# A second level of Strassen's algorithm in one GEMM of a retention + feed-forward kernel, with its weights streamed in 256 KB pieces

## The chip, the cores and the metric

The kernel runs on one core of one Trainium2 chip, in fp32. The metric is the device time of one execution in microseconds (us). "Span" is the time between the first and the last record of a profiled execution; it is 2 to 3 us shorter than the time of the same run.

TensorE does the matrix products; the trace lists each of its matmuls with a load of one operand, the weight, as an instruction of its own. In this kernel VectorE and ScalarE do the elementwise work, GpSimd a little of it, and SyncE issues the DMA transfers. The products are added up in buffers named banks (of the memory PSUM), and the program lets a bank be written again only when whoever reads it is done.

## The reference, cut to what matters

```python
def _attn_ref(q, k, v):                      # B, H, S, D = 4, 8, 768, 64
    for t in range(S):
        state = gamma * state + np.einsum('bhd,bhe->bhde', k[:, :, t], v[:, :, t])
        y[:, :, t] = scale * np.einsum('bhd,bhde->bhe', q[:, :, t], state)
    return y
def _moe_ref(x, w_in, w_out):                # x: 3072 x 512
    h = x @ w_in                             # 512 x 2048: the first GEMM
    g = np.where(h > 0.0, h, np.exp(np.minimum(h, 0.0)) - 1.0)      # ELU
    return g @ w_out                         # 2048 x 512: the second GEMM
```

The retention's output y, with its heads side by side, is x.

## The kernel before

The 3072 tokens go through in six blocks of 512. Block 1 (`tb = 0`) does its two GEMMs plainly. Blocks 2 to 6 do both with one level of Strassen's algorithm (in Winograd's form): a product of 2 x 2 quarters takes 7 multiplications of quarters for 8, and pays with additions. Sums of weights are formed once, sums of tokens for every block.

One generator serves both GEMMs. It interleaves the 7 products with their additions. `kept` is a ScalarE copy out of PSUM, `plus` a VectorE addition of PSUM and a kept copy:

```python
def strassen(product, use, between):
    yield
    pa = bank("a")                  # two banks "a", one "b", one "d"
    product(1, pa, True)
    m1 = kept(pa)
    yield
    pb = bank("b")
    product(2, pb, True)
    use("C11", plus(pb, m1))
    yield
    product(6, pa, False)           # accumulates on product 1
    u2 = kept(pa)
    yield
    pd = bank("d")
    product(7, pd, True)
    yield
    product(5, pa, False)
    u4 = kept(pa)
    use("C22", plus(pd, u4))
    yield "gap"
    product(3, pa, False)
    use("C12", pa)
    yield
    product(4, pd, False)           # on the same bank d
    use("C21", plus(pd, u2))
```

In the second GEMM a product is 16 matmuls of 128 x 128 weights and 256 columns. Its weights, already combined, come from a scratch in DRAM, 1 MB at a time, through three buffers. In the first GEMM, `use` is the ELU: two ScalarE activations and one VectorE operation.

```python
def second(tb, gqs):
    def product(j, ps, begin):
        name = {1: "C11", 2: "C21", 3: "C22", 4: "C11", 5: "T1", 6: "C11", 7: "T3"}[j]
        ws = fetched.pop((tb, j))
        for f in range(NF):                                        # 8
            for d in range(2):
                nc.tensor.matmul(
                    ps[:, d, :], lhsT=ws[:, f, d * P : (d + 1) * P], rhs=gqs[f // 2][name][:, f % 2, :],
                    ...
                )
        ...   # fetch the weights three products ahead; update C11 after products 2 and 6
```

The next block's retention runs in the gaps between these products: five bursts of small TensorE work (64 x 64 matmuls), namely scores, states and three steps of outputs. The scores are 128 such passes, which run four abreast. The first product is emitted before the last two products of the first GEMM (`tail`), so that TensorE does not wait for the last ELU.

## Time and profile before

The time before is 676.14 us, the median of three runs (674.76 to 676.36).

| before | value |
|---|---|
| span of the profiled run | 672.2 us |
| TensorE busy, and share of the chain that ended last | 97%, 97% |
| VectorE busy | 47% |
| mean DMA rate | 140 GB/s |
| one product of the second GEMM | 6.91 us, 7 in a block |
| TensorE's wait for another engine in blocks 3 to 6 | one, at the very end |

The prediction shows the lines. The end of a matmul in the profile is modelled, so busy time and the bracket "[idle before]" understate a stop by the modelled tail. Where a stop's length matters, I take the start of one matmul to the start of the next and subtract the usual pace; this I call start to start.

### The profile page before, as it was taken

The page shows a single profiled execution, that of the slowest core. Times are in us where ns is not written, and L with a number is a line of the kernel's source. Part 1 is how long each engine was busy: PE and PEld are TensorE (multiplying, and loading weights), DVE is VectorE, ACT ScalarE, POOL GpSimd, SP SyncE. Part 2 cuts the span into 40 slices and gives each one's busy share as a digit, 9 for nine tenths or more (in the row PEclk, how much of TensorE's full clock was granted, in tenths as well). Part 3 has the DMA queues.
Part 4 walks back from the last instruction along what each step waited for, and adds up shares of the span by engine and source line. Part 5 has one row for each costly group of instructions (what it writes and reads, how often), then busy time and mean ns, then how long its engine had stood idle before and what let it go on. Part 6 is the DMA issues. An engine that isn't in the chain of part 4 may idle for free.

```text
span 672.2 us, 12402 instructions
## 1 busy us (share of the span) xinstructions
PE 654.7 (97%) x5472; PEld 530.3 (79%) x5472; DVE 319.0 (47%) x529; ACT 209.1 (31%) x336; POOL 25.2 (4%) x28
## 2 busy tenths in 40 slices
PE   4899999999999999999999999999999999999997
PEld 4664445458888888888888888888888888888886
DVE  5698688566736224445313554503443612444400
ACT  7477642015540004441002542001453100444100
POOL 1001100001100001100000200000200000000000
PEclk9899999999999999999999999999999999999999
DMA  8547967249003458003347301445601335200441
GB/s 342 224 157 288 345 212 262 116 149 385 29 25 118 128 157 326 4 0 108 119 128 281 119 0 63 142 141 162 247 0 59 91 121 157 79 1 0 140 127 47
DMA packets 51941, 94.12 MB, mean 140 GB/s; under 512 B 2224, under 2 KB 39088, under 8 KB 49840
## 3 DMA queue, kind: packets, MB, share of 16 engines
q1 hardware_dynamic: 51888, 93.33, 40.5%
q8 instruction: 43, 0.70, 0.4%
q14 instruction: 10, 0.08, 0.0%
HBM read 78.64 MB, written 14.68 MB: 139 GB/s over the span
## 4 chain that ended last, share of the span: by engine, by line
PE 97%; DMA 1%; DVE 0%; issue 0%; SPq 0%; ACT 0%
PE pa L516 21%; PE pa L480 21%; PE pd L516 11%; PE pd L480 10%; PE hp L379 6%; PE pb L516 5%; PE pb L480 5%; PE pa L395 4%; PE kv L268 2%; PE pb L395 2%; PE pd L395 2%; PE y L316 2%; PE y L292 2%; PE sc L246 2%; PE pa L366 1%; DMA qk<-in_qkv_dram 1%
## 5 line engine op out<-in xcount | busy, mean ns | idle before, releaser
L516 PE MATMUL pa<-g,ws 128*128 128x256 f32 x640 | 142.8, 381 | 0.7 <-ACT m L432 0.7
L437 DVE TENSOR_TENSOR h<-pd,m 128x512 f32<-128x512 f32 x50 | 34.6, 692 | 215.8 <-ACT m L432 137.6
L516 PEld LDWEIGHTS pa<-g,ws 128*128 128x128 f32 x640 | 120.5, 190 | 17.8 <-ACT m L432 1.1
L432 ACT COPY m<-pa 128x512 f32<-128x512 f32 x75 | 43.3, 578 | 263.2 <-PE pa L516 170.4
L516 PE MATMUL pd<-g,ws 128*128 128x256 f32 x320 | 71.5, 382 | 0.0
L516 PEld LDWEIGHTS pd<-g,ws 128*128 128x128 f32 x320 | 60.1, 190 | 8.4
L355 ACT ACTIVATE r<-r 128x512 f32<-128x512 f32 x96 | 60.7, 632 | 3.1
L354 ACT ACTIVATE r<-h 128x512 f32<-128x512 f32 x60 | 37.9, 632 | 61.8 <-DVE h L437 61.8
L357 DVE SCALAR_TENSOR_TENSOR g<-r,h 128x512 f32<-128x512 f32 x60 | 42.7, 712 | 14.5 <-ACT r L355 14.5
L220 POOL TENSOR_TENSOR kvn<-kvn,vf 128x512 f32<-128x512 f32 x20 | 23.2, 1161 | 458.1 <-DMA kvn<-in_qkv_dram 314.1
L480 PE MATMUL pa<-xb,w_a 128*128 128x256 f32 x160 | 37.8, 379 | 0.0
L480 PE MATMUL pd<-xt,w_s 128*128 128x256 f32 x160 | 37.8, 379 | 0.0
L480 PE MATMUL pa<-xb,w_s 128*128 128x256 f32 x160 | 37.8, 379 | 0.0
L480 PE MATMUL pb<-xb,w_a 128*128 128x256 f32 x160 | 37.8, 379 | 0.0
L480 PE MATMUL pa<-xt,w_s 128*128 128x256 f32 x160 | 37.8, 379 | 0.0
L480 PE MATMUL pa<-xt,w_b 128*128 128x256 f32 x160 | 37.8, 379 | 0.0
L480 PE MATMUL pd<-xt,w_b 128*128 128x256 f32 x160 | 37.8, 379 | 0.0
L516 PE MATMUL pb<-g,ws 128*128 128x256 f32 x160 | 35.3, 379 | 0.0
L480 PEld LDWEIGHTS pa<-xb,w_a 128*128 128x128 f32 x160 | 30.4, 190 | 4.6 <-issue 0.5
L480 PEld LDWEIGHTS pb<-xb,w_a 128*128 128x128 f32 x160 | 30.4, 190 | 4.1
L480 PEld LDWEIGHTS pa<-xt,w_b 128*128 128x128 f32 x160 | 30.4, 190 | 4.1
L480 PEld LDWEIGHTS pd<-xt,w_b 128*128 128x128 f32 x160 | 30.4, 190 | 4.1
(93 smaller groups left out, 744.0 us busy)
## 6 DMA issues: line engine op xcount, KB each, us to landing
ws<-scratch_dram SPq DMA_DIRECT2D x35, 1024.0 KB, 5.8
wraw<-in_w_dram SPq DMA_DIRECT2D x16, 1024.0 KB, 5.7
qk<-in_qkv_dram SPq DMA_DIRECT2D x24, 512.0 KB, 9.2
kvn<-in_qkv_dram SPq DMA_DIRECT2D x24, 512.0 KB, 9.2
out_dram<-h SPq DMA_DIRECT2D x20, 256.0 KB, 5.8
scratch_dram<-w_s SPq DMA_DIRECT2D x8, 512.0 KB, 7.1
scratch_dram<-so SPq DMA_DIRECT2D x8, 512.0 KB, 3.6
out_dram<-ot SPq DMA_DIRECT2D x4, 256.0 KB, 2.2
```

The costliest lines, as they stand in the source:

```text
L220: eng.tensor_tensor(out=kv[:, 1], in0=kv[:, 1], in1=vf[:, i].unsqueeze(2).to_broadcast([C, H, D]), op=ALU.mult)
L246: nc.tensor.matmul(sc[a][rows(sub), x, p, :], lhsT=qk[rows(a), 1, p, rows(sub)], rhs=qk[rows(a), 0, p, rows(sub)], start=True, stop=True, ...
L268: nc.tensor.matmul(kvs[sub][rows(a), x, p, :], lhsT=kv[rows(sub), 0, 2 * p + a, :], rhs=kv[rows(sub), 1, 2 * p + a, :], start=True, stop=T ...
L354: nc.scalar.activation(r, h, AF.Relu, scale=-1.0)
L355: nc.scalar.activation(r, r, AF.Exp, scale=-1.0)
L357: later.append(lambda: nc.vector.scalar_tensor_tensor(g, r, -1.0, h, ALU.add, ALU.max))
L379: nc.tensor.matmul(hp, lhsT=w[n][:, fi, j // 2, j % 2, :], rhs=xb[:, j, :], start=(j == 0), stop=(j == 3))
L395: nc.tensor.matmul(ops[d], lhsT=wo[:, row, d * P : (d + 1) * P], rhs=gs[row * NF + f], start=(f == 0 and row == 0), stop=(f == NF - 1 and ...
L432: nc.scalar.copy(m, ps)
L437: nc.vector.tensor_tensor(out=h, in0=ps, in1=m, op=ALU.add)
L480: nc.tensor.matmul(ps[:, fi, :], lhsT=w[:, fi, j2, :], rhs=x[:, j2, :], start=(begin and fi == 0 and j2 == 0), stop=(j2 == 1), skip_group_ ...
L516: nc.tensor.matmul(ps[:, d, :], lhsT=ws[:, f, d * P : (d + 1) * P], rhs=gqs[f // 2][name][:, f % 2, :], start=(begin and f == 0 and d == 0 ...
```

## The change

The intent is to apply Strassen's idea once more, inside each of the 7 products of the second GEMM, from the third block on: 49 small products of 4 matmuls with 128 columns. That is 392 passes of TensorE in place of 224 passes of twice the width. VectorE and ScalarE pay for it with sums of operands and of results. In block 2 the kernel forms the sums of weights once and stores them to a second scratch. Then the 49 weight pieces of every block are streamed, 256 KB each, through eleven buffers.

```diff
+    def combine_w_out(j, ws):                       # in block 2 only, once for each product
+        a11, a21, a12, a22 = (ws[:, 4 * k : 4 * k + 4, P * d : P * d + P] for k in range(2) for d in range(2))
+        s12, s34 = (t4.tile([P, 2, 4, P], FP32, name="so", tag="t4") for _ in range(2))
+        tt(s12[:, 0], a21, a22, ALU.add)
...
+            nc.sync.dma_start(
+                scratch2[j - 1, :, 1024 * k : 1024 * k + 1024], x.rearrange("p k f d -> p (k f d)")
+            )
+    RING = 11
+    def fetch_small():
+        tb, j, k = to_fetch.pop(0)
+        t = ring.tile([P, 4, P], FP32, name="wq", tag="wq")
+        if k in (1, 2, 4):                          # pieces that are plain weights
...
+            nc.sync.dma_start(t, scratch[f : f + 4, :, col : col + P].rearrange("f p d -> p f d"))
+        else:
+            nc.sync.dma_start(t.rearrange("p f d -> p (f d)"), scratch2[j - 1, :, 512 * n : 512 * n + 512])
+    def second_twice(tb, behind_last):
+        def inputs(j):                              # VectorE: sums of operands of product j
+            sub(t[:, 0], b12, b11)
+            sub(t[:, 1], b22, t[:, 0])
+            sub(t[:, 2], b22, b12)
+            sub(t[:, 3], b21, t[:, 1])
...
+        def inner(j):                               # the seven small products of product j
+            product(j, 1, pa, True)
+            m1 = copy(pa)                           # ScalarE
+            product(j, 2, pb, True)
+            add(res[:, 0, 0], pb, m1)               # VectorE
+            yield
+            product(j, 6, pa, False)
+            u2 = copy(pa)
+            product(j, 7, pd, True)
+            product(j, 5, pa, False)
+            add(res[:, 1, 1], pd, copy(pa))
+            yield
+            product(j, 3, pa, False)
+            nc.scalar.copy(res[:, 0, 1], pa)
+            product(j, 4, pd, False)
+            add(res[:, 1, 0], pd, u2)
+            sum_up(j, ...)                          # VectorE: the outer sums
...
+        for at, j in enumerate(ORDER2):
+            cur = inner(j)
+            next(cur)                               # (j, 1), (j, 2)
+            if j == 1:
+                yield "tail"                        # the first GEMM's last two products
+            for _ in before:                        # (j-1, 3), (j-1, 4)
+                pass
+            if j == 2:
+                next_input(2)                       # the update of C11
+            if j == 5:
+                next_input(6)
+            if at + 1 < 7:
+                inputs(ORDER2[at + 1])
+            else:
+                behind_last()
+            next(cur)                               # (j, 6), (j, 7), (j, 5)
+            before = cur
+            yield j                                 # a burst of the next block's retention
```

Below, (j, k) is the small product k of the product j; j-1 is the product before j in the order 1, 2, 6, 7, 5, 3, 4. The pool of 20 buffers for ELU results also became fixed tiles.

## The prediction

> **What bounds the kernel now.** I read the engine shares and the chain first, to learn which engine sets the end; then the groups by form, for durations; then the timeline and the windows, for the pace. The page of the kernel before, engine shares and chain:
>
> ```profile
> PE 654.7 (97%) x5472; PEld 530.3 (79%) x5472; DVE 319.0 (47%) x529; ACT 209.1 (31%) x336; POOL 25.2 (4%) x28
> ...
> PE 97%; DMA 1%; DVE 0%; issue 0%; SPq 0%; ACT 0%
> ```
>
> TensorE carries 97% of the span and 97% of the chain, so only less PE time, or a new PE wait, moves the end. Groups by form (busy us, mean ns, then idle before them):
>
> ```profile
> L516 PE MATMUL pa<-g,ws 128*128 128x256 f32 x640 | 142.8, 381 | 0.7 <-ACT m L432 0.7
> L516 PEld LDWEIGHTS pa<-g,ws 128*128 128x128 f32 x640 | 120.5, 190 | 17.8 <-ACT m L432 1.1
> ...
> L437 DVE TENSOR_TENSOR h<-pd,m 128x512 f32<-128x512 f32 x50 | 34.6, 692 | 215.8 <-ACT m L432 137.6 <-PE pd L480 44.6 <-PE pd L516 33.6
> ...
> L279 DVE TENSOR_TENSOR xt<-kv,xt 128x256 f32<-128x256 f32 x32 | 13.6, 424 | 2.2 <-ACT xt L277 0.8
> ```
>
> L516 is the second GEMM. Its pa, pb and pd rows hold 640+160+320 = 1120 matmuls; the code issues 5 blocks x 7 products x 16 = 560. So one fp32 matmul is two passes, each with its own weight load. The mean of 381 ns is not the pace, since passes overlap. That is read off the timeline, here the first with PE alone, the second with weight loads alone:
>
> ```profile
> 315.01 2.10 PE L246 MATMUL sc<-qk 64*64 64x64 f32 x128
> 317.04 7.17 PE L516 MATMUL pa<-g,ws 128*128 128x256 f32 x32
> ```
>
> ```profile
> 335.31 0.30 PEld L516 LDWEIGHTS pa<-g,ws 128*128 128x128 f32 x2
> ```
>
> A product of 32 passes that follows another takes 6.91 us in the chain in order of time, so **216 ns per pass**; block by block the second GEMM costs 7 x 6.91 = 48.4 us. The windows of one block's second part (retention of the next block woven in) and of a first part:
>
> ```profile
> 208.90:252.80 43.90, 43.90 (x659) 38.14 (x658) 12.51 (x25) 1.76 (x3) 0.00 (x0) 1.00 0.46 139
> 252.80:304.60 51.80, 51.80 (x242) 45.60 (x241) 23.93 (x36) 23.50 (x40) 4.36 (x4) 1.00 0.29 107
> ```
>
> The columns are window, length, then busy us of PE, PEld, DVE, ACT, POOL. In the second part VectorE works 12.5 of 43.9 us. It has plenty of room today, and PE has no gap at all.
>
> **What the Trainium skill says.** "TensorE: Matmul & The Clock Gate", Back-to-back issue gap, says that in a stream of weight load and matmul pairs the spacing is set by both, and that narrow matmuls feel it: 81 ns at 128 columns where an isolated one needs 56. The trace cannot test 128 columns; at 256 the loads (190 ns each) hide inside the 216 ns pace, as PE shows no gap. "Perfetto Trace Analysis", Optimizing Tensor Performance, Matmuls: larger matmuls are more efficient than smaller ones. The change goes the other way. "DMA: Bandwidth & Descriptors", Bandwidth, gives 0.95 us for 64 KB and 6.15 us for 1 MB. The trace has 5.8 us for 1 MB of ws and 2.2 us for 256 KB of out<-ot, which agrees.
>
> **Part 1, matmuls: the gain.** In blocks 3 to 6 of six (tb = 2..5) each of the 7 products becomes 7 smaller ones of 4 matmuls with 128 columns: 49 x 4 x 2 = 392 passes for 7 x 16 x 2 = 224. Break-even is 48.4 us / 392 = 123 ns per pass. What is the pace at 128 columns? Matmul: 216 = 256 columns at 0.833 ns (213.3) + 2.5, so 128 columns need 109. Weight load: in the last fence two loads of 128 columns span 0.30 us, 190 of which is the second, so the second began about 0.11 us after the first; the loads overlap one another. The 64-column matmuls tell whether load and matmul of equal width really run side by side: 128 passes in four quadrants follow the product at 315.01 and give way at 317.04, 2.03 us for 32 waves, 63 ns with the changeover; the individual starts in the steady part are 58 ns apart, which is 53.3 + 5. I therefore take 106.7 + 5 = **112 ns** (estimate), and 392 x 0.1117 = 43.8 us. Gain 4.6 us per block, **18.2 us for four blocks**. A one-to-one split would give 7/8; 12.5% of 48.4 is 6.0, and the narrower pass eats 1.5 of it.
>
> **Part 2, VectorE: what it costs.** Per block the second part now holds: 7 x 4 operand subtractions of 128x512 at 0.69 = 19.3; three PSUM adds of 128x128 per product, 21 x 0.29 (from 424 at 256 and 692 at 512: 156 + 1.05 ns per element) = 6.1; outer sums 7 x 0.69 = 4.8; the update of C11, 8 x 0.69 = 5.5 (as before); the next block's retention and combine_x, some 12. That is 48 us beside about 52 us of PE (43.8 + 8.2 of retention matmuls). VectorE goes from 28% of the window to over 90%. It does not become the bound in sum, but it works in order, and the PSUM bank d is released by adds queued behind long work. I laid the queue out by hand, taking 0.89 us per small product, 0.2 us until its result can be read, 0.27 us for the ScalarE copy.
> - Normal step: after product (j-1,4), 0.2 + 0.29 + 0.69 + 2.75 (inputs of the next product) + 0.33 = 4.3 us until bank d may be accumulated on again; PE has 6 products = 5.35 us of other work. No stall.
> - Start of the part: the copy of u2 sits behind two ELU activations of the first GEMM's last tile (stall 0.75), and inputs(2) waits for that tile, so (1,4) waits 0.7. **1.4 us**.
> - Second product, with the C11 update (2.75 more) and then four score masks (2.7): (6,7) waits 0.5. Before (4,7) the xb multiplies (2.7) hold the queue: 0.75. **1.3 us**.
> - The last block has no retention to hide behind: the C11 update leaves 6.3 against 5.35 twice, plus 0.25 from three sums: 2.2 + 1.4 = **3.6 us**.
> Sum: 3 x 2.7 + 3.6 = 11.7 us. The end of the program gains two more waits on one bank and one more add, 0.8 us.
>
> **Part 3, weights.** 49 pieces of 256 KB per block are 12.8 MB for 7.3 MB before, fetched as a buffer falls free, eleven deep. In a stretch without retention PE eats one per 0.89 us, 294 GB/s. In the timeline's busiest stretches the ws loads (1 KB packets) ran at 383 GB/s by the windows view. Pieces that come from the first scratch have 512-byte packets, three in seven, so I put the mix near 330 (estimate from the per-packet times of 84 ns for 2 KB and 46 ns for 1 KB). Ten pieces of lead are 8.9 us against 2.2 us of landing plus at most 3 us in which the queue stands behind an output store. **Hidden.**
>
> **Part 4, the one-time cost.** Block 2 adds 28 combining subtractions (19.4 us of VectorE in a window where it is mostly idle) and 7 MB of stores; the ring is filled during the following first GEMM, 48 us. Nothing on the path. Fixed tiles in place of the 20-buffer pool: the built order shows waits by region (the middle of a product waits for the last tile's ELU), so no stall in the first GEMM.
>
> **Sum.** 676.1 - 18.2 + 11.7 + 0.8 = **670.4 us**, ratio 0.991.
>
> **Rivals.**
> 1. VectorE's queue stalls less than I laid out, because the pieces shift and slack grows: only the fixed start of 1.4 us per block stays. Then 676.1 - 18.2 + 6.4 = 664. For it: small products give six products of slack. Against: 48 of 52 us busy leaves no room for the retention's bursts.
> 2. Weight loads do not hide at 128 columns. At 123 ns per pass nothing is gained in the matmuls, giving 689 with the stalls; at the load's full 190 ns it would be 74.5 us per block, +104 us, 790. Against the extreme: the two loads within 0.30 us and the 64-column waves.
> 3. The weight stream falls behind (small packets, one in-order queue that also waits for output stores). If PE ran at 250 GB/s in the second part, a piece takes 1.05 us, 51.4 us per block: +3 us instead of -4.6, some 690. Against: eleven buffers, and retention work that gives 8 us per block to catch up.
>
> **Range and chances.** The pace (109 to 114 ns) moves the time by -4 to +4 us; the stalls by -6 to +7. I predict 670 us, range 661 to 681. Faster by over 2% needs 662.6, so stalls under 5 us: chance 0.14. Slower by over 2% needs rival 2 or 3: 0.07. Within 2%: 0.79.
>
> **What would show it.** In the profile after: eight passes per small product starting 0.89 us apart (right) or 1.0 and more (rival 2); PE idle before the new matmuls of 10 to 14 us, released by VectorE adds and ScalarE copies (right) or by DMA into wq (rival 3); VectorE near 90% busy in the second part. I am wrong if the PE gaps are under 5 us, or if the small products run at another pace while nothing waits.

## The result, and the profile after

The changed kernel takes 666.62 us, the median of four runs (665.87 to 668.91), beside 675.45 us for the kernel before. The ratio is **0.9875** (95% interval 0.9846 to 0.9904): within 2%, and 3.4 us under the predicted 670. All ratios here divide the mean time of one kernel's runs by that of the other's runs of the same rounds, so they are not quite the ratios of the quoted medians.

Lines of the page of the changed kernel, in the order of the page: engine shares, the chain, the new matmuls with idle time, the weight stream.

```profile
PE 640.9 (96%) x6144; PEld 538.9 (81%) x6144; DVE 434.7 (65%) x769; ACT 228.3 (34%) x432; POOL 23.7 (4%) x28
...
PE 87%; DVE 8%; issue 2%; DMA 1%; ACT 0%; SPq 0%; DVEq 0%
...
L611 PE MATMUL pd<-ts,wq 128*128 128x128 f32 x448 | 60.3, 278 | 0.6 <-DVE res L623 0.3
L611 PE MATMUL pa<-ts,wq 128*128 128x128 f32 x448 | 59.6, 276 | 1.3 <-ACT ms L619 1.3
...
wq<-scratch_dram SPq DMA_DIRECT2D x196, 256.0 KB, 4.2
```

VectorE has gained 115.7 us of work and TensorE has lost 13.8. The chain now runs 8% of its way through VectorE, and 2% through "issue": time in which TensorE waited for nothing that the profile knows. Before, that share was 0%.

The timeline of TensorE in block 3 shows what happened. The first columns are start and length; the bracket is the idle time before, and what ended it.

```profile
303.21 1.05 PE L611 MATMUL pa<-ts,wq 128*128 128x128 f32 x8
304.16 1.16 PE L611 MATMUL pd<-ts,wq 128*128 128x128 f32 x8
305.64 1.16 PE L611 MATMUL pa<-ts,wq 128*128 128x128 f32 x8 [0.32 <-ACT ms L619]
306.63 1.06 PE L611 MATMUL pa<-gC,wq 128*128 128x128 f32 x8
307.53 1.06 PE L611 MATMUL pb<-gC,wq 128*128 128x128 f32 x8
308.42 1.06 PE L611 MATMUL pa<-gC,wq 128*128 128x128 f32 x8
309.54 1.16 PE L611 MATMUL pd<-ts,wq 128*128 128x128 f32 x8
...
313.31 1.73 PE L261 MATMUL sc<-qk 64*64 64x64 f32 x101
315.65 0.68 PE L261 MATMUL sc<-qk 64*64 64x64 f32 x27 [0.61 <-issue]
```

Three things are to be seen.
1. **The pace.** From 306.63 to 307.53 to 308.42 the small products start 0.893 us apart: 8 passes of 111.6 ns.
2. **The start of the part.** (1,5) starts at 305.64, which is 1.48 us after (1,7) at 304.16: 0.48 us late beyond the 1.0 us of a product whose first weight load does not hide (some 0.10 us). It awaited the copy of u2. Then (1,4) starts at 309.54, 1.12 us after its predecessor: 0.23 us late, waiting for the addition that frees bank d. Three of the products there have such an unhidden first load (0.10 us each), and (1,7) itself starts 0.06 us late, 0.36 us together.
3. **A stop that nothing explains.** The 128 scores passes of the burst, which before took 2.10 us in one piece, break off after 101 and go on 0.61 us later ("issue"; 0.77 us start to start). There are five such stops in the profile, all in retention bursts or just after one: 0.77, 0.96, 0.87, 1.19 and 0.76 us, **4.5 us** in all. The profile before has none.

Where the copy of u2 stood is seen in ScalarE's timeline of the same kernel, and the pace of VectorE in its own:

```profile
304.14 0.63 ACT L369 ACTIVATE r<-h 128x512 f32<-128x512 f32 x1 [1.19 <-DVE h L448]
304.80 0.63 ACT L370 ACTIVATE r<-r 128x512 f32<-128x512 f32 x1
305.34 0.25 ACT L619 COPY ms<-pa 128x128 f32<-128x128 f32 x1
...
310.95 2.49 DVE L526 TENSOR_TENSOR gC<-gT,gC 128x512 f32<-128x512 f32 x4
```

The copy (L619) runs behind two ELU activations of the first GEMM's last tile, and these waited 1.19 us for a VectorE sum. In the last line four VectorE operations of 128 x 512 take 2.49 us together, 0.62 us each with the end of the last one counted in. From start to start such operations of the changed kernel, one behind the other, are **0.60 to 0.61 us** apart, although the listing gives one of them 0.69.

### The profile page after: what moved, and what is told of

The parts are those of the page before. It is cut to its first block, busy times and chain, and to the rows that moved or that the text cites. A ratio compares the mean times of both kernels' runs of the same rounds, so it can differ in the third digit from the quotient of the medians.

```text
span 664.6 us, 14658 instructions
## 1 busy us (share of the span) xinstructions
PE 640.9 (96%) x6144; PEld 538.9 (81%) x6144; DVE 434.7 (65%) x769; ACT 228.3 (34%) x432; POOL 23.7 (4%) x28
## 4 chain that ended last, share of the span: by engine, by line
PE 87%; DVE 8%; issue 2%; DMA 1%; ACT 0%; SPq 0%; DVEq 0%
PE pa L491 20%; PE pa L611 12%; PE pd L491 9%; PE pd L611 7%; PE hp L392 6%; PE pb L491 5%; PE pa L406 4%; PE pa L547 4%; DVE ts L600 3%; PE pb L611 2%; PE pd L547 2%; PE pb L406 2%; PE pd L406 2%; PE y L331 2%; PE sc L261 2%
## 5 line engine op out<-in xcount | busy, mean ns | idle before, releaser
L619 ACT COPY ms<-pa 128x128 f32<-128x128 f32 x84 | 22.2, 264 | 123.7 <-PE pa L611 119.1
L611 PE MATMUL pd<-ts,wq 128*128 128x128 f32 x448 | 60.3, 278 | 0.6 <-DVE res L623 0.3
L611 PE MATMUL pa<-ts,wq 128*128 128x128 f32 x448 | 59.6, 276 | 1.3 <-ACT ms L619 1.3
L611 PEld LDWEIGHTS pa<-ts,wq 128*128 128x128 f32 x448 | 54.8, 192 | 2.2 <-ACT ms L619 2.0
L611 PEld LDWEIGHTS pd<-ts,wq 128*128 128x128 f32 x448 | 54.5, 192 | 2.3 <-DVE res L623 1.9
L611 PE MATMUL pa<-gC,wq 128*128 128x128 f32 x384 | 52.0, 278 | 0.4 <-ACT ms L619 0.4
L372 DVE SCALAR_TENSOR_TENSOR gC<-r,h 128x512 f32<-128x512 f32 x60 | 42.7, 712 | 10.3 <-ACT r L370 10.3
L611 PEld LDWEIGHTS pa<-gC,wq 128*128 128x128 f32 x384 | 47.2, 192 | 1.7 <-ACT ms L619 0.5
L623 DVE TENSOR_TENSOR res<-pd,ms 128x128 f32<-128x128 f32 x56 | 16.1, 287 | 33.7 <-PE pd L611 31.9
L491 PEld LDWEIGHTS pd<-xt,w_s 128*128 128x128 f32 x160 | 30.4, 190 | 4.1
```

The source lines that it names most:

```text
L372: later.append(lambda: nc.vector.scalar_tensor_tensor(g, r, -1.0, h, ALU.add, ALU.max))
L491: nc.tensor.matmul(ps[:, fi, :], lhsT=w[:, fi, j2, :], rhs=x[:, j2, :], start=(begin and fi == 0 and j2 == 0), stop=(j2 == 1), skip_group_ ...
L611: nc.tensor.matmul(ps, lhsT=w[:, f, :], rhs=ts[j][k][:, f, :], start=(begin and f == 0), stop=(f == 3), skip_group_check=True,)
L619: nc.scalar.copy(m, ps)
```

## The experiments

All of them edit the changed kernel, except before_traffic, which edits the kernel before. Two questions stood at the outset. What are the unexplained stops? The theory: TensorE consumes instructions at twice the rate (a small product of 8 matmuls with their 8 loads takes 0.893 us, so 256 instructions last 14.3 us; before, a product of 64 instructions took 6.91 us, so 256 lasted 27.6 us), and its fetch of instructions, a DMA transfer too, is held up by the weight stream. The DMA view of the kernel before and that of the changed kernel list an instruction queue q8 (packets, MB, share):

```profile
q8 instruction: 43, 0.70, 0.4%
```

```profile
q8 instruction: 49, 0.80, 0.5%
```

The packets are of 16 KB. TensorE has 11,036 records before and 12,499 after (matmuls, loads and its few control instructions), which is 257 and 255 to a packet. So I took q8 for TensorE's instruction fetch, some 256 instructions to a packet. At the outset this was an inference; the section on why the prediction was right, part 3, has what bears it out. A burst of 128 scores with their loads uses up 256 instructions in 2 us. The rivals: the stream alone, or the denser use of instructions alone. The second question was what the waits on ScalarE and VectorE are worth.

The results at a glance. "Stops" are stops over 0.3 us with no releaser, in the profiled run, start to start:

| run | ratio to before (95%) | stops | median us |
|---|---|---|---|
| the change | 0.9875 (0.9846, 0.9904) | 5, 4.5 us | 666.62 |
| no_stream (wrong result) | 0.9802 (0.9785, 0.9819) | 0 | 661.44 |
| before_traffic | 1.0029 (1.0012, 1.0046) | 0 | 676.38 |
| split_retention | 0.9883 (0.9867, 0.9900) | 0 | 666.61 |
| both_orders | 0.9944 (0.9919, 0.9969) | 4, 5.0 us | 670.99 |
| early_copy | 0.9881 (0.9864, 0.9898) | 3, 3.4 us | 666.43 |
| late_inputs | 0.9892 (0.9871, 0.9912) | 5, 6.7 us | 667.37 |
| tuned | **0.9781 (0.9767, 0.9796)** | 0 | 659.72 |
| ring6 | 1.0107 (1.0071, 1.0142) | 5, 9.1 us | 683.62 |
| tuned_unsplit | 0.9868 (0.9841, 0.9895) | 4, 5.4 us | 665.10 |
| big_packets | 0.9887 (0.9867, 0.9907) | 3, 3.1 us | 667.29 |
| tuned_big | 0.9859 (0.9842, 0.9876) | 3, 2.6 us | 665.56 |
| from_fourth | 0.9901 (0.9885, 0.9917) | 2, 1.6 us | 667.70 |

The rows fall into three groups that shared their runs of the kernel before (medians 675.09, 674.40 and 674.60 us): the four after the change; then early_copy, late_inputs, tuned and ring6; then the last four. All but no_stream gave correct results.

### no_stream: the same instructions without the weight stream

```diff
         tb, j, k = to_fetch.pop(0)
+        if len(kept_w) == RING:
+            small_w.append(((tb, j, k), kept_w[len(to_fetch) % RING]))
+            return
         t = ring.tile([P, 4, P], FP32, name="wq", tag="wq")
+        kept_w.append(t)
```

Only the first eleven pieces are fetched, and all 196 products use them. 185 transfers fall away, TensorE's instructions stay. The result is wrong (relative error 4.2).

> The changed kernel, but the eleven weight pieces fetched first serve all products of blocks 3 to 6 (the result is wrong on purpose; every matmul, subtraction and add is as in the changed kernel). 185 of 196 piece transfers are gone. In the profile of the changed kernel TensorE stops five times for 0.76 to 1.19 us (4.5 us in all), released by no other engine ('issue'), four of the five with a busy weight stream, each just after a 16 KB packet of the instruction queue. Theory A (the weight stream delays TensorE's instruction fetch): the five stops are gone, and the time is about 4.5 us under the changed kernel's, ratio to the kernel before near 0.981. Theory B (the stops come from TensorE's doubled instruction rate alone): they stay at 3 to 5 us and the ratio stays near 0.9875. Theory C (the pieces themselves arrive late, unseen): waits on DMA do not show in the profile, so this would show only as a time more than 5 us lower. A wrong result is expected.

The stops are gone, and the burst is whole again, as TensorE's timeline shows:

```profile
315.25 2.09 PE L261 MATMUL sc<-qk 64*64 64x64 f32 x128
317.27 1.16 PE L616 MATMUL pa<-gC,wq 128*128 128x128 f32 x8
```

The other waits are unchanged (0.48 us four times, 0.32 twice, 0.52 at the end). The ratio falls from 0.9875 to 0.9802, which is 4.9 us of 675, for 4.5 us of stops. The denser use of instructions alone makes no stops; the stream is needed for them.

### before_traffic: the kernel before, with traffic added

```diff
             ws = fetched.pop((tb, j))
+            if tb > 1:
+                for part in range(3):
+                    nc.sync.dma_start(
+                        spare[part, :, :].rearrange("p (a c) -> p a c", c=128),
+                        scratch[part, :, 0:1024].rearrange("p (a c) -> p a c", c=128),
+                    )
```

Each product of the second GEMM of blocks 3 to 6 adds three copies of 512 KB from DRAM to DRAM, in runs of 512 bytes.

> The kernel before, with three copies of 512 KB from HBM to HBM (512-byte runs) added in every product of the second GEMM from block 3 on, nothing waits for them: a stream beside its unchanged TensorE program. Theory A (a busy stream delays TensorE's instruction fetch): stops of 0.5 us and more released by 'issue' appear in the retention matmuls, which use up instructions fastest, 1 to 5 us in all, time up by 0.2 to 0.8%. Theory B (the doubled instruction rate is the cause): no such stop, time same within 0.2%. If the own weight fetches of 1 MB come late, waits on DMA would show, which would be another effect.

The windows view of 314 to 356 us, for the kernel before, for before_traffic and for the change. The columns are window, length, busy us of PE, PEld, DVE, ACT and POOL (instructions in brackets), granted clock, DMA share, GB/s:

```profile
314.00:356.00 42.00, 42.00 (x650) 36.34 (x649) 12.51 (x25) 2.13 (x4) 0.00 (x0) 1.00 0.47 142
```

```profile
314.00:356.00 42.00, 42.00 (x650) 36.33 (x649) 12.58 (x26) 2.13 (x4) 0.00 (x0) 1.00 0.87 287
```

```profile
314.00:356.00 42.00, 40.59 (x747) 39.48 (x739) 31.52 (x67) 5.49 (x21) 0.00 (x0) 1.00 0.76 227
```

At 287 GB/s and 87% DMA share, more than the change moves (227 GB/s, 76%), TensorE stays busy for the whole 42 us. The time rises by 0.3%, with no new stop: of the 1.5 us by which the profiled span is longer, 1.4 us come after the start of TensorE's last matmul. Traffic alone makes no stops either, as far as copies from DRAM to DRAM stand for the weight stream. Stream and denser use of instructions are needed together.

### split_retention: bursts of half the length

```diff
+            yield "half"                      # in second_twice, after (j-1, 3), (j-1, 4)
...
+                if j == "half":
+                    if step > 1:
+                        retention_half(tb + 1, step - 2, 1)
+                    continue
                 if step > 0:
-                    retention_step(tb + 1, step - 1)
+                    retention_half(tb + 1, step - 1, 0)
```

Each of the five steps is done in two halves, with three or four small products between them. The order of the matmuls on every bank stays, and the stream stays.

> The changed kernel with each retention step of the next block cut into its two halves, which are woven in some three small products apart: bursts of 64 narrow passes in place of 128. Theory A or B (TensorE uses up 256 instructions in 2 us during a burst and the next 16 KB of instructions are not there in time): half a burst leaves time to refill, the 'issue' stops shrink from 4.5 us to under 1.5 us; against that each extra change between narrow and wide matmuls costs 0.28 us, 15 of them 4.2 us, so the time stays within 1 us of the changed kernel, ratio 0.986 to 0.990. Rival (the stops have nothing to do with the burst): stops stay near 4.5 us, and the time is about 4 us above the changed kernel, ratio near 0.994.

The stops are gone (0 in the profile), and each half burst is whole, as TensorE's timeline of split_retention shows:

```profile
313.64 1.16 PE L261 MATMUL sc<-qk 64*64 64x64 f32 x64
...
318.50 1.16 PE L261 MATMUL sc<-qk 64*64 64x64 f32 x64
```

Yet the time is that of the change: 0.9883. The reason is a price that both kernels pay for each burst: the change to the small width and back costs 0.09 + 0.09 + 0.10 = 0.28 us, start to start. Fifteen more bursts (five in each of three blocks) cost 4.2 us, and 4.5 us of stops went. So the length of a burst is what starves TensorE, and splitting is worth its price only where it prevents a stop.

### both_orders: another TensorE order at the start, and later sums of operands

```diff
             u2 = copy(pa)
+            if j == 1:
+                yield
...
             if j == 1:
                 yield "tail"
+                next(cur)                    # (1, 6) between the tail's two products
+                yield "tail"
...
+            next(cur)                        # before inputs(...), for every j
             if at + 1 < 7:
                 inputs(ORDER2[at + 1])
...
-            next(cur)
```

The edit moves (1,6) and its copy between the last two products of the first GEMM, and for all seven products puts the sums of the next operands behind the additions that free the banks.

> The changed kernel with two changes of order and the same work. One: the first GEMM's last product is issued one small product later, so that the copy of u2 goes to ScalarE ahead of two ELU activations. Two: the four operand subtractions for the next product are issued after the add that releases bank d, not before it. Theory (the queued work behind which those two handovers stand costs about 0.8 us plus 0.35 us at the start of each of four blocks, and 0.43 + 0.43 + 0.27 us in the last block): 5 to 5.5 us less than the changed kernel, ratio to before about 0.979 to 0.981. Rival (the handovers only move: the subtractions now come late for the product that reads them): waits of TensorE on the subtraction appear instead and the ratio stays within 0.985 to 0.990.

This is a miss: 0.9944, some 4.7 us slower than the change. TensorE's timeline shows the wait that took the place of the one removed:

```profile
306.76 1.16 PE L611 MATMUL pd<-ts,wq 128*128 128x128 f32 x8 [0.79 <-DVE h L448]
```

Bank d, which the last product of the first GEMM fills, is wanted at once by (1,7), but VectorE has yet to read it: 0.95 us start to start, in all four blocks, where 0.48 and 0.23 were lost before. Three further waits of 0.41 to 0.42 us and one of 0.31 us arose elsewhere. These are not all of the 4.7 us; the rest is not assigned. One stop, now 2.08 us long, was followed by 3.4 us of half granted clock.

### early_copy and late_inputs: the two repairs one by one

early_copy leaves TensorE's order alone and only lets ScalarE copy u2 before the two ELU activations:

```diff
         product(4, pd, False)
+        yield                                # in strassen: the ELU of C21 is emitted later
         use("C21", plus(pd, u2))
...
             u2 = copy(pa)
+            if j == 1:
+                yield
...
             if j == 1:
+                yield "tail"
+                next(cur)                    # (1, 6)
                 yield "tail"
...
             next(cur)
+            next(tail)
+            next(tail)
+            next(cur)
             for _ in tail:
                 pass
```

> The changed kernel with one change of order: at the start of the second GEMM of blocks 3 to 6, ScalarE copies u2 before, not behind, the two ELU activations of the first GEMM's last tile; TensorE's order is untouched (in the run with both orders changed TensorE's order changed too, and bank d was then awaited for 0.95 us instead). Theory: the wait of 0.48 us plus the 0.10 us of unhidden weight load after it go, four times: 2.3 us less than the changed kernel in TensorE waits that the profile lists; in time 664.3, ratio 0.984, as far as the TensorE stops without a releaser (4 to 5 us, changing from run to run) allow. Rival (the ELU that now comes 0.3 us later holds up the inputs that follow): the wait returns as 0.3 us or more at the next handover of bank d, and the gain is under 1 us.

The wait moved, as the rival had it. The copy of u2 is no longer awaited, but (1,4) now waits for bank d, as TensorE's timeline of early_copy shows:

```profile
310.09 1.16 PE L612 MATMUL pd<-ts,wq 128*128 128x128 f32 x8 [0.66 <-DVE res L624]
```

That is 0.82 us start to start, four times, for 0.48 + 0.23 before. The time is that of the change (0.9881).

late_inputs puts the additions of (j,6), (j,7), (j,5) before the sums of the next operands, for j = 1, 2 and 5 alone:

```diff
+            late = j in (1, 2, 5)
+            if late:
+                next(cur)
             if at + 1 < 7:
...
-            next(cur)
+            if not late:
+                next(cur)
```

> The changed kernel with one change of order on VectorE: for products 1, 2 and 5 the four operand subtractions for the following product are issued behind the add that frees bank d, not ahead of it. Theory: the waits for bank d of 0.23 us (four blocks) and of 0.32, 0.32 and about 0.17 us (last block, two of them behind the C11 update) go, with 0.10 us each for the weight load after a wait: 1.3 + 0.8 us, or a little less, as the third of the last block is behind product 5's sums. About 2 us less than the changed kernel, ratio about 0.9845. Rival (the subtractions come late for their reader instead): new waits of TensorE on the subtractions, ratio 0.987 or more.

The 0.23 us waits of (1,4) and the two waits of 0.32 us in the last block are gone. Nothing was gained (0.9892): the stops grew to 6.7 us in the profiled run, the longest 2.36 us. The windows of that stop and of the 3.4 us after it:

```profile
312.00:316.00 4.00, 1.86 (x103) 1.60 (x102) 3.68 (x8) 0.27 (x1) 0.00 (x0) 1.00 0.82 250
316.00:319.40 3.40, 3.33 (x39) 3.22 (x40) 1.84 (x3) 0.27 (x1) 0.00 (x0) 0.57 0.05 12
```

In the first window TensorE works 1.86 of 4 us. In the second the granted clock is 0.57 (a mean: it was 0.50 from 316.48 to 319.89), and the DMA queue moves almost nothing, 12 GB/s. The stops thus vary between kernels and between executions (late_inputs spread from 663.84 to 668.71 us), and they mask gains of a microsecond or two.

### tuned: both repairs, and the three dense bursts split

The edits of early_copy and of late_inputs together, and split_retention's halves for scores, states and the first step of outputs only (128, 112 and 128 passes):

```diff
+        elif step == 2:
+            if pp == 0:
+                held["y"] = [outputs(tb, x) for x in range(2)]
+            next(held["y"][pp], None)
+        elif pp == 0:
+            outputs_step(tb, step - 2)
```

> The changed kernel with the early copy, the late inputs, and the three retention bursts of 128 passes split in halves (the two short ones left whole). Theory: 2.3 + 2.0 us of waits gone; the TensorE stops of 4.5 us without a releaser gone as in the fully split run, for 9 more changes of width at 0.28 us = 2.5 us. Sum -6.3 us against the changed kernel: 660 us, ratio 0.978, and TensorE waits over 0.13 us come to under 1.5 us in all, the last one (0.52 us, before the final pair of products) among them. Rival (the waits move): sum of TensorE excess stays over 12 us and the ratio over 0.984.

It takes **659.72 us** (659.52 to 659.97), ratio **0.9781**: over 2% faster than the kernel before, and faster than the change in every run. Lines from its page (engine shares and the chain), then its TensorE timeline:

```profile
PE 638.9 (97%) x6144; PEld 538.2 (82%) x6144; DVE 437.5 (67%) x769; ACT 228.4 (35%) x432; POOL 24.1 (4%) x28
...
PE 96%; DMA 1%; DVE 1%; issue 0%; SPq 0%; ACT 0%; DVEq 0%
```

```profile
302.38 1.16 PE L612 MATMUL pd<-ts,wq 128*128 128x128 f32 x8
303.37 1.06 PE L612 MATMUL pa<-ts,wq 128*128 128x128 f32 x8
...
310.61 1.16 PE L261 MATMUL sc<-qk 64*64 64x64 f32 x64
311.71 1.16 PE L612 MATMUL pa<-gC,wq 128*128 128x128 f32 x8
...
315.47 1.16 PE L261 MATMUL sc<-qk 64*64 64x64 f32 x64
```

The chain is again TensorE's (96%), "issue" has left it, the product after 302.38 follows at the normal pace, and the scores come in two bursts of 64, each whole. From block 3 on the only wait over 0.3 us left is one of 0.52 us near the end. Beside split_retention (0.9883), which splits without the repairs, tuned is 6.9 us faster. Six bursts fewer account for 1.7 us of that, so by estimate the repairs are worth some 5 us once there are no stops.

### tuned_unsplit: is the splitting needed?

This is tuned without the splitting, that is early_copy and late_inputs together.

> The tuned kernel with the retention bursts whole again, that is the changed kernel with both orders of work changed. Theory: the ScalarE and VectorE waits (early copy and late inputs together) stay away, as in the tuned kernel, and the TensorE stops without a releaser come back, 3 to 7 us of them, minus 2.5 us of changes of width: 662 to 664 us, ratio 0.981 to 0.985. Rival (the gain of the tuned kernel came all from the splitting, since each order alone gained nothing): ratio 0.987 or more.

It gives 0.9868, so the two repairs alone are hardly worth anything beside the change's 0.9875. The stops are back: four, 5.4 us, the longest 2.41 us and followed by half clock. TensorE's timeline of tuned_unsplit has that one in the burst of states:

```profile
531.41 0.68 PE L283 MATMUL kv<-kvn 64*64 64x64 f32 x17 [2.25 <-issue]
```

Its six runs spread from 662.48 to 669.74 us, where tuned's four lie within 0.5 us. The splitting is worth 0.9868 against 0.9781, some 6 us, although it adds nine changes of width (2.5 us).

### ring6: six buffers

```diff
-    RING = 11
+    RING = 6
```

> The changed kernel with 6 weight buffers in place of 11. Theory (the stream has 8.9 us of lead and needs landing 4.2 us as measured, plus up to 3 us behind an output store): five products of lead are 4.5 us, so the pieces behind a store and some others come late: 5 to 25 us more than the changed kernel, TensorE waiting for DMA into the weight buffers. Rival (the stream has room to spare even at half the buffers): within 2 us of the changed kernel, ratio 0.986 to 0.990. If it is as fast or faster, fewer buffers also mean a shallower queue, and the stops without a releaser may shrink.

It gives 1.0107, some 16 us slower than the change. From the waits of ring6 (us in all, times, longest), and from its timeline of TensorE:

```profile
PE pd L611 <- DMA wq<-scratch_dram: 5.5, 5, 2.7
...
PE pa L611 <- DMA wq<-scratch_dram: 2.4, 3, 1.1
```

```profile
356.12 1.13 PE L611 MATMUL pd<-ts,wq 128*128 128x128 f32 x8 [2.68 <-DMA wq<-scratch_dram]
```

TensorE now waits for weights, which it does not do with eleven buffers. So a late piece does show in the profile, other than theory C of no_stream had it. Stops without a releaser grew as well, up to 3.2 us. The eleven buffers are needed; the transfers are hidden by them and not in themselves.

### big_packets and tuned_big: is it the number of packets?

```diff
+        for n, x in enumerate((a11, a12, a22)):        # in combine_w_out
+            nc.sync.dma_start(
+                scratch2[j - 1, :, 2048 + 512 * n : 2560 + 512 * n].rearrange("p (f d) -> p f d", d=P), x
+            )
...
-            nc.sync.dma_start(t, scratch[f : f + 4, :, col : col + P].rearrange("f p d -> p f d"))
...
+        n = {5: 0, 6: 1, 7: 2, 3: 3, 1: 4, 2: 5, 4: 6}[k]
+        nc.sync.dma_start(t.rearrange("p f d -> p (f d)"), scratch2[j - 1, :, 512 * n : 512 * n + 512])
```

The plain pieces too are stored to the second scratch in block 2, so that every piece is fetched in packets of 2 KB in place of 512 bytes for three pieces in seven. big_packets does this to the change, tuned_big to tuned_unsplit.

> The changed kernel with its weight pieces 1, 2 and 4 copied once, in block 2, into the second scratch, so that all 196 fetches have 2 KB packets in place of 84 with 512-byte packets (43008 packets become 10752); bytes per block are the same. Theory A1 (the number of packets of the stream is what delays the instruction fetch): the stops without a releaser fall from 4.5 us to under 1.5 us and the time to 662 to 664 us, ratio 0.982 to 0.984. Theory A2 (the bytes, or any busy queue, do it): stops stay at 3 us or more, ratio 0.986 to 0.990. The 21 added stores of 256 KB in block 2 should cost nothing.

> Both orders changed, bursts whole, and 2 KB packets. Under A1 no stops and no added changes of width: 657 to 659 us, ratio 0.974 to 0.976, under the tuned kernel's 0.978. Under A2: like the run with both orders and whole bursts, 0.981 to 0.985.

They give 0.9887 and 0.9859, with 3 stops of 3.1 us and 3 of 2.6 us. So the stops do not need the small packets, though the packets' number may bear on their size. The edit brought a cost that I had not expected. TensorE's timeline of big_packets, at the end of block 2:

```profile
249.11 7.17 PE L551 MATMUL pd<-gC,ws 128*128 128x256 f32 x32 [1.99 <-DMA ws<-scratch_dram]
```

The added stores stand in the one in-order queue before the fetch of the last product's weights, and TensorE waits 1.99 us (2.69 in tuned_big, where 3.4 us of half clock followed, 1.7 us more). Without this, by estimate from the profiled runs, big_packets would be some 2 us faster and tuned_big some 4.5 us, which leaves it about 1 us behind tuned. Bigger packets without the added wait were not tried.

### from_fourth: the second level one block later

```diff
-    to_fetch = [(tb, j, k) for tb in range(2, NTB) for j, k in USE]
+    to_fetch = [(tb, j, k) for tb in range(3, NTB) for j, k in USE]
...
-        if tb == 1:
+        if tb <= 2:
             cur = second(tb)
```

> The changed kernel with the second level only from the fourth block on, so in three blocks in place of four; the third block runs as in the kernel before. From the trace one block gains 4 x 8 x 49 x 0.1116 = 43.7 us in place of 48.4, 4.7 us, and gives back 1.1 us at its start and 1.5 us of stops on average. So 2 us more than the changed kernel: 668.8 us, ratio 0.990 to 0.992. Rival (the third block gained nothing, as it has two of the five stops): ratio stays at 0.987 to 0.988.

It gives 0.9901, 1.8 us slower than the change (the two intervals overlap, so the size is uncertain): one block of the second level nets about 1.8 us of the 4.6 us that its matmuls save. Four such blocks make 7 us, most of the 8.8 us of the change; the last block has no bursts and gives back less.

## Why the prediction was right, and where not

The time was 3.4 us from the prediction. Two errors of the sum partly cancel, so that it came so near is in part luck, and one of its own marks of being wrong was met. For blocks 3 to 6, start to start, in us of TensorE time:

| term | predicted | measured |
|---|---|---|
| matmuls: 4 x (48.36 - 43.76) | -18.2 | -18.4 |
| start of the part, four times | 4 x 1.4 = 5.6 | 4 x (0.48 + 0.23 + 0.36) = 4.3 |
| middle of blocks 3 to 5 | 3 x 1.3 = 3.9 | 0 |
| middle of the last block | 2.2 | 0.32 + 0.32 + 0.17 + 3 x 0.10 = 1.1 |
| end of the program, more than before | 0.8 | 0.62 - 0.94 = -0.3 |
| stops without a releaser | 0 | 4.5 |
| sum | -5.7 | -8.8 |

The spans of the two profiled runs differ by 7.6 us and the medians by 8.8. Of the 1.2 us between 8.8 and 7.6, 0.3 had arisen before block 3, 0.4 is scattered within the bursts, 0.2 comes after the start of the last matmul, and the rest is not assigned.

**Part 1, the matmuls: right.** The estimate of 112 ns met 111.6, and rival 2 (weight loads that do not hide) falls. The prediction read the pace from two overlapping loads and from the 64-column waves. The mean duration of the new matmuls, 276 to 278 ns, would have told nothing of the pace.

**Part 2, VectorE: the mechanism was right, the sizes were not.** The start stalls where it was said to, on the copy behind the ELU activations and then on bank d. The mis-sized term is **0.69 us for each VectorE operation of 128 x 512**. That is the mean of single records, and records of operations in a row overlap. The pace is 0.60 to 0.61 us. It could have been read before the change, nearly, by dividing the busy time by the count: one group of the kernel before, from its groups by form, shows it, beside one of the new operations in the changed kernel:

```profile
L528 DVE TENSOR_TENSOR g<-g 128x512 f32<-128x512 f32 x20 | 12.5, 684 | 0.0
```

```profile
L600 DVE TENSOR_TENSOR ts<-gC,ts 128x512 f32<-128x512 f32 x48 | 33.0, 688 | 0.8
```

12.5 us for 20 is 0.625 us, with the end of the last of each row counted in (0.60 from start to start), while the mean beside it says 684 ns. A chain of 8 or 9 such operations was thus put some 0.7 us too long. In the middle of blocks 3 to 5 the predicted waits of 0.5 and 0.75 us vanish with that. In the last block two waits of 0.95 us became 0.32, shorter by about as much. VectorE was said to be over 90% busy in the second part. The windows view of the changed kernel, from the first operand sums to the end of the part, and from the first burst on:

```profile
297.98:355.73 57.75, 55.96 (x889) 53.87 (x888) 45.26 (x90) 11.39 (x34) 0.00 (x0) 1.00 0.70 208
...
313.20:355.70 42.50, 41.09 (x778) 39.89 (x777) 32.02 (x67) 5.68 (x21) 0.00 (x0) 1.00 0.77 227
```

That is 45.26 of 57.75 us (78%) and 32.02 of 42.5 (75%). Rival 1, VectorE's queue stalling less than laid out, therefore came nearer for this part: about 5.1 us net in place of 12.5 (rival 1 had 6.4). The prediction called itself wrong if the gaps were under 5 us. Those released by VectorE and ScalarE were: 4.2 us from start to start without the unhidden loads after them, 1.9 us by the idle times of the profile.

The Trainium skill had the right figure too. "Vector Engine (DVE) Microarchitecture Reference", 5.2 Measured stream behaviour on trn2, gives 1.0417 ns per column plus about 75 ns per instruction once queued (measured there on streams of 32-bit integers). By estimate from this, 512 columns take 608 ns; the trace agrees, with 0.60 to 0.61 us in fp32. The prediction didn't look there.

**Part 3, the weights: right for the buffers, wrong in the landing time, and it missed the side effect.** A piece took 4.2 us from issue to landing where 2.2 was used, and was hidden all the same. No small product of the changed kernel waits for weights, and ring6 shows what the margin is worth. But the sum has no term for what the stream does to TensorE's own supply. In its place stand the five stops, 4.5 us. No_stream, before_traffic and split_retention together show that they need the stream, the changed kernel's instructions and the long bursts, all three.

What is held up can be read from the kept traces, although they name no releaser. The 34 stops of the nine profiles that have any lie at only five places of TensorE's program: after 5313, 6081, 7616, 8385 and 10,176 of its records, to within one. These places are 3, 6, 3 and 7 times 256 records apart, to within one. The last packet of q8 to end before TensorE went on was the 20th, 23rd, 29th, 32nd and 39th there, in every profile; so these too are 3, 6, 3 and 7 apart. And TensorE went on 0.99 to 1.62 us after the end of that packet, whether the stop was of 0.4 or of 3.2 us; in 11 of the 34 the packet ended only after the stop had begun. In late_inputs, for one, the last matmul before the stop began at 313.64, the packet ended at 314.44, and TensorE went on at 316.07. So what TensorE waits for is the next block of 256 instructions; this rests on the agreement of place and time. It also explains, by inference, why removing other waits gained so little in kernels with stops: TensorE comes earlier to a place that it can't pass before the packet. What makes the packets late beside the stream, and what fills the microsecond or more after their end, stays open.

**Part 4, the one-time cost: right** for the changed kernel. Block 2's 28 combinations and 7 MB of stores brought TensorE no wait. For further stores this did not hold, as big_packets found.

So the cancellation was this: VectorE's waits were put 7.4 us too high, and 4.5 us of stops were not foreseen. A sum right on VectorE alone would have said 663, which is 3.6 us too low. (Rival 3's 690 leaves out the stalls of the sum: with them it would be some 700. It did not come about.)

## What to carry to other kernels

To size the queue of an engine that works in order, take start-to-start times, or busy time divided by count, and never the mean duration of one record: some 14% per operation decided here whether a bank was free in time. When a change shortens TensorE's instructions and adds a stream of transfers, look for stops marked "issue" in dense bursts of tiny matmuls, and split the bursts (nine splits cost 2.5 us here, and the stops that they did away with were 5.4 us in the profile of tuned_unsplit). Repair waits together and check each alone: two repairs that gained nothing measurable without the splitting were part of a version that is 1% faster with it.

## What the Trainium skill lacked or had wrong

- **Instruction fetch.** "Runtime: NRT & Kernel Launch", Instruction fetch mechanics, says that fetching 16 KB blocks is mostly hidden, because instructions are dispatched more slowly than they are fetched. This case is an exception: at the boundaries of such blocks TensorE stopped five times for 0.76 to 1.19 us (4.5 us of 664.6) where bursts use 256 instructions in 2 us beside a stream of 227 GB/s, and went on 0.99 to 1.62 us after the packet's end. There was no stop without the stream or with halved bursts.
- **The clock after a stop.** "TensorE: Matmul & The Clock Gate", Part 1, puts the half clock after an idle window of about 3.4 us. Here the granted clock was 0.5 for 3.4 us after a stop of only 2.08, 2.13, 2.36 and 2.41 us (both_orders, early_copy, late_inputs, tuned_unsplit), from 0.4 to 1.1 us after its end. Two stops of 2.10 and 2.25 us in ring6 were not followed by it, and none up to 1.6 us was.
- **The fp32 pace.** The section on the back-to-back gap of "TensorE: Matmul & The Clock Gate", which the prediction quotes, names no pace for fp32 (other pages speak of the number of passes alone). Here an fp32 matmul is two passes, each with a 128 x 128 weight load, at 216 ns per pass of 256 columns and 111.6 ns per pass of 128, where the section has 81.
- **Change of width.** No page gives its length: 0.28 us for a burst of 64 x 64 matmuls between full ones (0.09 going in, 0.09 + 0.10 coming out), in both kernels.
- **Landing in a stream.** The table of "DMA: Bandwidth & Descriptors" that the prediction quotes is for transfers issued by GpSimd and gives no time to landing within a stream of others. Here 256 KB landed in 2.2 us in block 1 (output stores of the kernel before) and in a median of 4.2 us within the stream of 196 pieces (loads, so the comparison is rough).
